# Top-k attention and a two-layer network on one core: the mask's ReLUs, GpSimd's joins and the end keys' transposes change places within a step

## The chip, the cores and the metric

The kernel runs on one core of a Trainium2 chip. The core's engines work side by side, each through its own queue in program order: TensorE (PE, matrix products and transposes; its weight loads are listed as PEld), VectorE (DVE), ScalarE (ACT), GpSimd (POOL) and SyncE (SP), whose queue issues nearly all DMAs. An instruction waits at the head of its engine's queue until the semaphores that it needs have come, and everything behind it waits too. The time is that of one execution on the device, in microseconds; lower is better. Three runs of the kernel before gave 1617.61, 1620.12 and 1620.48 us, median 1620.12.

## What is computed

Attention that keeps, for each query, only the 32 largest of 576 scores, then a normalised two-layer network with a residual, on 8 batches, 8 heads, 576 positions and head dimension 64. The weights of the network come as 64-bit floats.

```python
scores = scale * np.matmul(q, k.transpose(0, 1, 3, 2))
kth = np.partition(scores, -top_k, axis=-1)[..., -top_k:-top_k + 1]
scores = np.where(scores >= kth, scores, -1000000000.0)
attn = np.exp(scores - np.max(scores, axis=-1, keepdims=True))
attn = attn / (np.sum(attn, axis=-1, keepdims=True) + 1e-09)
x = np.matmul(attn, v)                      # heads side by side: (8, 576, 512)
mu = np.mean(x, axis=-1, keepdims=True)
var = np.mean((x - mu) ** 2, axis=-1, keepdims=True)
xn = (x - mu) / np.sqrt(var + 1e-06) * g_ln
out = x + np.maximum(xn @ w_ch1, 0.0) @ w_ch2   # 512 -> 2048 -> 512
```

## The kernel before

**Units.** The heads are taken in pairs. A unit is 128 queries of one pair: two tiles of 128 x 576 scores, one for each head. The last 64 of the 576 queries make a rest unit: one tile, with the two heads one above the other. There are 160 units, 32 of them rest units. A group is the two or three units of one job (batch, head pair, query tiles) that share a product with the values.

**Steps.** The main loop runs over steps n = 0 to 166, and in one step parts of several units are issued, so that a unit passes through five or six steps. In step n:

- PE makes the scores of unit n+2 (`scores`, `score_half`, L402) into four PSUM buffers of the pool `ps` (two for a rest unit); ACT copies them to SBUF (L383, tile `sc`).
- DVE selects in unit n (`select`, L431 to L445): the 576 columns were folded into 288 maxima and 288 minima (`halve`, L423 and L424, at the end of the step before); four rounds of eight largest find the 32nd largest.
- ACT masks unit n-1: two small instructions prepare bias and edge (`prepare`, L457 and L458), then for each of the two tiles a steep ReLU of edge minus score (L494), from which POOL subtracts the score (L497). Both write the tile `e`, of which there are two buffers. A masked place is now huge, and the exponential (`weigh`, L505, ACT) of its negative is zero.
- The exponentials are turned so that keys lie on partitions: units that are not the last of their group by DVE in blocks and by DMA through HBM (`move`, L536, unit n-2), the others by PE (`turn`, L563). The 64 keys per head that do not fill a block of 128, the end keys, are always turned by PE (`turn_ends`, L596, for rest units L592 and L593): for a moved unit three steps after its selection, n-3. That transpose is the last reader of `e`, so unit n-1's ReLU, which takes the same buffer, waits for it.
- PE multiplies a finished group with the values (`values`, L629 and L636), ACT copies (`take_values`, L644), PE transposes back (`place`, L671), ACT scales into the rows x (L648).

**Places in PSUM.** The pool `ps` has five buffers in rotation, for scores, transposes and value products alike; a new tile waits until the fifth before it has been read out. The network's products have three buffers of their own.

**The network.** Its work stands in a list `todo` and is dealt out by `fill()`, called some eight times in a step, by costs written into the program, not by what the chip does: hidden products (L776, ReLU at L799 on ACT) and second products (L815 for the first block, L933 for the others). The other blocks use seven products in place of eight on quarters of the matrices, for which POOL adds and subtracts quarters of the hidden values (L863 to L869) and, once, of the second weight matrix. These are the forms: four pairs (`form_pair`, L987 to L990, four tensor operations each), written to HBM (`keep_pair`), and fetched from there (L1003). They begin when the first block is done (`plain_done`), one pair a step; second products of the other blocks may be dealt out in steps after the one in which the last pair was kept (`formed`).

**Converting the weights.** In steps -1 to 20 the 32 pieces of 128 x 512 64-bit numbers become 32-bit: one or two pieces a step, four ahead of step 0. `split`: ACT takes size, low bits and sign (L163, L165, L168), POOL clamps the size (L164) and scales signs of the first matrix by the gain (L170). `shift` (DVE, L176) moves the size's bits. `join` (POOL, L182 and L184) adds the low bits and multiplies by the sign. The pieces split in one step are shifted and joined in the next; a piece may be used from the step after its join.

**The note.** `watch` (POOL, L464) notes whether eight minima were enough for each unit. Where they were not, a second program follows; here it doesn't run.

**Order in a step, before.** Program order, which is each engine's queue order:

1. scores of n+2 with ACT's copies, values of a group, maxima round 0;
2. the first half of the weights' work, a `fill()`, the end keys' transpose of n-3, `prepare` and the first tile's mask of n-1, a `fill()`, the second tile's mask (in steps 0 to 8 both masks come before the weights and the exponentials right behind);
3. copies of values and of end keys, transposes, rounds 1 to 3, exponentials, four more `fill()`;
4. after round 3: the note of unit n, halving of n+1, shifts and joins of the pieces split in step n-1, splits of step n, a pair of forms.

Of the kernel before, what the change touches and what calls it, by code (L numbers as in the profile page):

```python
# [29 lines left out]
def compute(  # L30
# [67 lines left out]
    def turned():  # L98
        return brief("tp")
# [110 lines left out]
    def weights(n, phase):  # L210

        now, before = batches.get(n, []), batches.get(n - 1, [])
        coming = batches.get(n + 1, [])
        if phase == 0:
            for x in coming if n < LATE else []:
                x.fetch()
            for x in now[0::2] if n < LATE else []:
                x.split()  # L220
        elif phase == 1:
            for x in before:
                x.shift()
            for x in before:
                x.join()
            for x in now if n >= LATE else now[1::2]:
                x.split()
            for x in coming if n >= LATE else []:
                x.fetch()

    todo = []
    share = [0.0]
# [143 lines left out]

    def scores(u):

        u.sc = scpool.tile([P, 2, S], FP32, tag="sc", name="sc")
        made = [score_half(u, s) for s in range(2)]  # L380
        for t in range(len(u.tiles)):
            for s in range(2):
                nc.scalar.copy(  # L383
                    u.sc[:, t, s * HALF : (s + 1) * HALF], made[s][t][:, 0:HALF]
                )

    def score_half(u, s):
# [23 lines left out]
    def halve(u):  # L411

        nt = len(u.tiles)
        u.lo = lopool.tile([P, 2, HALF], FP32, tag="lo", name="lo")
        u.hi = hipool.tile([P, 2, HALF + 8 * low_rounds], FP32, tag="hi", name="hi")  # L420
        a, b = u.sc[:, 0:nt, 0:HALF], u.sc[:, 0:nt, HALF:S]
        lo, hi = u.lo[:, 0:nt], u.hi[:, 0:nt, 0:HALF]
        nc.vector.tensor_tensor(hi, a, b, ALU.max)  # L423
        nc.vector.tensor_tensor(lo, a, b, ALU.min)  # L424
# [158 lines left out]
        heads = () if u.moved else range(len(u.tiles))  # L583
        return [lambda t=t: part(t) for t in heads] + [last]

    def turn_ends(u):

        q0 = place_of(u) * 32
        g = u.group
        ps = turned()  # L590
        if u.rest:
            nc.tensor.transpose(ps[0:R, 0:P], u.e[:, 0, JP:S], ident[:])  # L592
            nc.tensor.transpose(ps[:, P : 2 * P], u.e[:, 0, JP - R : S], ident[:])  # L593
        else:
            ends_e = u.e[:].rearrange("p t n -> p (t n)")[:, JP : JP + P]
            nc.tensor.transpose(ps[:, 0:P], ends_e, ident[:])  # L596

        def copy():
            if u.rest:
                for h in range(2):  # L600
                    nc.scalar.copy(  # L601
                        g.pt[h * R : (h + 1) * R, 2 * J, q0 : q0 + R],
                        ps[h * R : (h + 1) * R, h * (P + R) : h * (P + R) + R],
                    )
            else:
                nc.scalar.copy(g.pt[:, 2 * J, q0 : q0 + P], ps[:, 0:P])

        return copy
# [494 lines left out]
    def at(i):  # L1103
        return units[i] if 0 <= i < N else None
# [94 lines left out]
    nc.sync.dma_start(grow[:], g_ln.rearrange("(c p) -> c p", p=P))  # L1199
    load(fresh[1], nc.sync, nc.scalar)  # L1200
    scores(units[0])
    halve(units[0])
    scores(units[1])
    load_gain()
    weights(-1, 0)
    weights(-1, 1)
    for n in range(END):
# [20 lines left out]
        if quick:  # L1228
            values(g)
            take_values(g)  # L1230
        for x in ahead:
            scores(x)
        if g and not quick:
            values(g)
        if n in brings:
# [14 lines left out]
        if doubt is not None and at(n - 2) and at(n - 2).ends_watch:  # L1250
            settle_watch(at(n - 2).half)
            if n == N + 1:
                tell()
        if early:
            prepare(ex)
            for t in range(2):
                mask(ex, t)
            weights(n, 0)
            for t in range(2):
                weigh(ex, t)  # L1260
        if not early:
            weights(n, 0)
        fill()
        turned_before = at(n - 3)
        if turned_before and turned_before.moved:
            late_ends = turn_ends(turned_before)
        if mk and not early:
            prepare(mk)
            mask(mk, 0)
        fill()  # L1270
        if mk and len(mk.tiles) > 1 and not early:
            mask(mk, 1)
        if g and not quick:
            take_values(g)
        if late_ends:
# [17 lines left out]
                load(fresh[later], nc.sync, nc.sync, n >= EARLY)  # L1293
        if n == 0:
            scores(units[2])
        for x in (u if n < EARLY else None, mk if n > EARLY else None):
            if x and x is units[x.job.last]:
                load_values(x.job)
                ends_due[n + 1] = x.job
# [33 lines left out]
        fill()  # L1333
        if u:
            select(u, 3)
            if doubt is not None:
                watch(u)
        if nxt:
            halve(nxt)
        weights(n, 1)  # L1340
        if g and not quick and g.job.hp == NHP - 1:
            for qt in g.qts:
                if qt < J:
                    arrived(n, (g.job.b, qt), xs[g.job.b, qt])
        if plain_done[0] is not None and plain_done[0] < n:
            if made_pair:
                keep_pair(made_pair.pop())
            if pairs_left:
                made_pair.append(form_pair(pairs_left.pop(0)))
        if late and late.job.hp == NHP - 1:  # L1350
            r = late.job.b // 2
            if r % 2:
# [61 lines left out]
```

## Time and profile before

| | |
|---|---|
| three runs, median (lowest to highest) | 1620.12 us (1617.61 to 1620.48) |
| profiled execution: its own time, its span | 1619.01 us, 1617.1 us |
| PE, matmuls | 1482.7 us busy (92%), 7770 instructions |
| DVE | 1411.5 us (87%), 3971 |
| ACT | 1072.8 us (66%), 2984 |
| POOL | 1071.2 us (66%), 1489 |
| mean granted TensorE clock | 0.971 |
| subtractions L497 on POOL | 288, mean 1466 ns |
| ReLUs L494 on ACT | 288, mean 769 ns |
| score copies L383 on ACT | 576, mean 408 ns |
| halving L423 and L424 on DVE | 160 each, mean 967 and 1030 ns |

Busy shares are means over the whole span. An engine can be busy while another is what the end waits for, and the stretches of the run differ: until about 21 steps in, weights are converted; then the forms are made; then attention and the network run together; and at the end only the network is left. The profile counts two matmul rows for each product of the program (L776: 2304 rows).

### The profile page before, as it was taken

What the parts mean: (1) busy time and instruction counts of PE and PEld (TensorE: products, weight loads), DVE (VectorE), ACT (ScalarE), POOL (GpSimd) and SP (SyncE); (2) the same over time, 40 slices, a digit from 0 to 9 for tenths busy, and PEclk for the clock granted to TensorE, in tenths of its full rate; (3) what the DMA queues carried; (4) which work ended last, traced back from release to release, by engine and by line L of the source; (5) the groups of instructions that cost most, each with busy time, mean ns of one, the idle gap of its engine ahead of it and who ended that gap; (6) DMA issues with size and microseconds to landing.
All of it is one profiled execution on the core that took longest, in us unless ns stands there. A gap on an engine that the chain in (4) does not pass through costs nothing.

```text
span 1617.1 us, 27069 instructions
## 1 busy us (share of the span) xinstructions
PE 1482.7 (92%) x7770; PEld 1119.5 (69%) x7770; DVE 1411.5 (87%) x3971; ACT 1072.8 (66%) x2984; POOL 1071.2 (66%) x1489
## 2 busy tenths in 40 slices
PE   3568778699979999999999999999999999999997
PEld 1336446467757677777777777777777777778886
DVE  7979888999999999999999999999999999991000
ACT  5877776477767786776766867677667776754221
POOL 6768886766646666677765758576757675746244
PEclk9879999899989999999999999999999999999999
DMA  8424664544646556545564556545555555522211
GB/s 205 123 70 137 174 164 125 156 125 130 182 130 180 154 151 171 161 150 134 163 188 137 140 148 176 162 126 170 146 173 149 136 154 162 164 83 86 73 33 54
DMA packets 367205, 228.27 MB, mean 141 GB/s; under 512 B 248772, under 2 KB 337352, under 8 KB 367048
## 3 DMA queue, kind: packets, MB, share of 16 engines
q1 hardware_dynamic: 362312, 225.86, 49.1%
q8 instruction: 64, 1.05, 0.3%
q10 hardware_dynamic: 4736, 0.59, 0.2%
q14 instruction: 93, 0.76, 0.2%
HBM read 154.01 MB, written 72.35 MB: 140 GB/s over the span
## 4 chain that ended last, share of the span: by engine, by line
PE 70%; POOL 10%; DVE 9%; ACT 6%; DMA 2%; issue 1%; SPq 0%; ACTq 0%; POOLq 0%; DVEq 0%
PE hps L776 26%; PE ops L933 22%; PE scps L402 8%; PE av L629 6%; POOL e L497 3%; DVE m L445 3%; DVE hi L431 2%; PE tp L563 2%; PE av L636 2%; POOL w L184 2%; POOL wt L182 1%; ACT e L494 1%; ACT e L505 1%; ACT sc L383 1%; DVE sc L536 1%
## 5 line engine op out<-in xcount | busy, mean ns | idle before, releaser
L497 POOL TENSOR_TENSOR e<-e,sc 128x576 f32<-128x576 f32 x288 | 417.0, 1466 | 366.9 <-ACT e L494 366.6
L776 PE MATMUL hps<-xT,w 128*128 128x256 f32 x2304 | 550.9, 387 | 13.8 <-ACT xT L738 9.0
L776 PEld LDWEIGHTS hps<-xT,w 128*128 128x128 f32 x2304 | 427.8, 193 | 91.5 <-issue 16.5
L445 DVE MAX8 m<-hi 128x8 f32<-128x296 f32 (+1 forms) x1152 | 469.9, 442 | 0.1
L431 DVE MATCH_REPLACE8 hi<-m,hi 128x288 f32<-128x288 f32 (+1 forms) x864 | 377.2, 441 | 0.0
L933 PE MATMUL ops<-w,h 128*128 128x256 f32 x1360 | 326.0, 384 | 8.9 <-DMA w<-forms 7.8
L505 ACT ACTIVATE e<-e,m 128x576 f32<-128x576 f32 x288 | 224.6, 780 | 129.1 <-POOL e L497 127.6
L933 PEld LDWEIGHTS ops<-w,h 128*128 128x128 f32 x1360 | 250.2, 192 | 52.1 <-issue 8.7
L494 ACT ACTIVATE e<-sc,m 128x576 f32<-128x576 f32 x288 | 211.9, 769 | 91.8 <-PE tp L596 91.5
L383 ACT COPY sc<-scps 128x288 f32<-128x288 f32 x576 | 198.4, 408 | 89.8 <-PE scps L402 57.9
L424 DVE TENSOR_TENSOR lo<-sc 128x576 f32<-128x576 f32 (+1 forms) x160 | 164.9, 1030 | 0.0
L423 DVE TENSOR_TENSOR hi<-sc 128x576 f32<-128x576 f32 (+1 forms) x160 | 154.7, 967 | 8.9 <-ACT sc L383 4.8
L799 ACT ACTIVATE h<-hps 128x512 f32<-128x512 f32 x144 | 85.6, 595 | 96.7 <-PE hps L776 96.2
L629 PE MATMUL av<-pt,vb 128*64 128x256 f32 (+2 forms) x1088 | 142.3, 404 | 2.8 <-ACT pt L601 2.1
L536 DVE STREAM_TRANSPOSE sc<-e 128x512 f32<-128x512 f32 x176 | 114.7, 685 | 31.5 <-POOL e L497 18.9
L933 PE MATMUL ops<-wt,s 128*128 128x256 f32 x544 | 130.1, 381 | 0.0
L402 PE MATMUL scps<-kT,late_qT 64*128 64x288 f32 (+3 forms) x832 | 122.5, 411 | 1.4 <-ACT x L648 1.1
L437 DVE MAX8 hi<-lo 128x8 f32<-128x288 f32 x288 | 117.5, 443 | 0.0
L402 PE MATMUL scps<-kT,qT 64*128 64x288 f32 x512 | 95.1, 467 | 21.5 <-DVE qT L332 11.8
L629 PEld LDWEIGHTS av<-pt,vb 128*64 128x64 f32 x1088 | 72.2, 139 | 59.7 <-issue 12.8
L933 PEld LDWEIGHTS ops<-wt,s 128*128 128x128 f32 x544 | 99.1, 190 | 16.5 <-issue 3.1
L563 PE MATMUL tp<-ident,e 128*128 128x128 f32 x448 | 72.8, 290 | 40.6 <-ACT e L505 40.4
(104 smaller groups left out, 1852.0 us busy)
## 6 DMA issues: line engine op xcount, KB each, us to landing
turned<-sc SPq DMA_DIRECT2D x88, 512.0 KB, 2.9
pt<-turned SPq DMA_DIRECT2D x352, 128.0 KB, 2.8
w<-forms SPq DMA_DIRECT2D x136, 256.0 KB, 4.2
vb<-in_v_dram SPq DMA_DIRECT2D x68, 288.0 KB, 3.9
raw<-in_moe_w_ch_dram SPq DMA_DIRECT2D x32, 512.0 KB, 5.1
kT<-kept SPq DMA_DIRECT2D x36, 288.0 KB, 3.3
kin<-in_k_dram SPq DMA_DIRECT2D x128, 72.0 KB, 2.7
kept<-kT SPq DMA_DIRECT2D x32, 288.0 KB, 3.1
```

Source lines behind the costliest of these rows:

```text
L383: nc.scalar.copy(u.sc[:, t, s * HALF : (s + 1) * HALF], made[s][t][:, 0:HALF])
L402: nc.tensor.matmul(ps[i * R : i * R + ql, o : o + width], qT[r, q0 : q0 + ql], kT[r, k0 : k0 + width], start=True, stop=True,)
L423: nc.vector.tensor_tensor(hi, a, b, ALU.max)
L424: nc.vector.tensor_tensor(lo, a, b, ALU.min)
L431: nc.vector.match_replace(x, m[:, t, :], x, LOWEST)
L445: nc.vector.max(m[:, t, :], u.hi[:, t, 0:width])
L494: nc.scalar.activation(u.e[:, t], u.sc[:, t], AF.Relu, bias=u.edge[:, t : t + 1], scale=-STEEP)
L497: nc.gpsimd.tensor_tensor(u.e[:, t], u.e[:, t], u.sc[:, t], ALU.subtract)
L505: nc.scalar.activation(u.e[:, t], u.e[:, t], AF.Exp, bias=u.bias[:, t : t + 1], scale=-scale, accum_out=g.den[:, col : col + 1],)
L629: nc.tensor.matmul(av[h * D : (h + 1) * D, 0 : g.nq], vb[:, h * (J + 1) + c, :], g.blocks[:, h, 0 : g.nq // 32, c, :], start=(c == 0), sto ...
L776: nc.tensor.matmul(ps[0][:, side * N : (side + 1) * N], w1[:, c, f * P : (f + 1) * P], self.xT[:, c, 0:N], start=(c == 0), stop=(c == NC - 1),
L933: nc.tensor.matmul(bank[name][:, 0:Q], a(j), rhs, start=first and j == 0, stop=(j == G - 1), skip_group_check=not first,)
```

## The change

Within a step, four things change places. The amount of arithmetic stays the same.

- The score copies are split off (`take_scores`) and stand behind the masks. Both tiles' masks, with `prepare`, stand at the step's head, right behind the scores' matmuls, in all steps.
- The end keys' transpose of unit n-3 comes right behind the scores and writes into columns 288 to 415 of the first score buffer, of which the scores use only 288, in place of a buffer of its own. Where a step makes no scores, it takes one as before.
- The shifts go from the end of step n to its head, ahead of round 0; the joins, the note (of unit n-1 now, one step later) and a pair of forms stand behind the subtractions of n-1. The condition for forms becomes `plain_done < n - 1`.
- The first half of the weights' work stands behind all of these.

```diff
         elif phase == 1:
-            for x in before:
-                x.shift()
-            for x in before:
-                x.join()
             for x in now if n >= LATE else now[1::2]:
                 x.split()
...
+    def join_weights(n):
+        for x in batches.get(n - 1, []):
+            x.join()
...
     def scores(u):
+        u.made = [score_half(u, s) for s in range(2)]
+        return u.made[0][0][:, HALF:]
+
+    def take_scores(u):
         u.sc = scpool.tile([P, 2, S], FP32, tag="sc", name="sc")
-        made = [score_half(u, s) for s in range(2)]
...
-    def turn_ends(u):
+    def turn_ends(u, ps=None):
...
-        ps = turned()
+        if ps is None:
+            ps = turned()
...
+        for x in batches.get(n - 1, []):
+            x.shift()
+        spare = None
         for x in ahead:
-            scores(x)
+            spare = scores(x)
+        turned_before = at(n - 3)
+        if turned_before and turned_before.moved:
+            late_ends = turn_ends(turned_before, spare)
+        if mk:
+            prepare(mk)
+            for t in range(len(mk.tiles)):
+                mask(mk, t)
+        join_weights(n)
+        if mk and doubt is not None:
+            watch(mk)
+        if plain_done[0] is not None and plain_done[0] < n - 1:
+            if made_pair:
+                keep_pair(made_pair.pop())
+            if pairs_left:
+                made_pair.append(form_pair(pairs_left.pop(0)))
+        for x in ahead:
+            take_scores(x)
         if g and not quick:
             values(g)
...
+        weights(n, 0)
         if early:
-            prepare(ex)
-            for t in range(2):
-                mask(ex, t)
-            weights(n, 0)
             for t in range(2):
                 weigh(ex, t)
-        if not early:
-            weights(n, 0)
         fill()
-        turned_before = at(n - 3)
-        if turned_before and turned_before.moved:
-            late_ends = turn_ends(turned_before)
-        if mk and not early:
-            prepare(mk)
-            mask(mk, 0)
         fill()
-        if mk and len(mk.tiles) > 1 and not early:
-            mask(mk, 1)
...
             select(u, 3)
-            if doubt is not None:
-                watch(u)
...
-        if plain_done[0] is not None and plain_done[0] < n:
-            if made_pair:
-                keep_pair(made_pair.pop())
-            if pairs_left:
-                made_pair.append(form_pair(pairs_left.pop(0)))
```

The calls of `scores` outside the loop's head are each followed by `take_scores`.

More of the change, by code (lines that the diff above doesn't have):

```diff
@@ L210, in weights @@
     def weights(n, phase):
-        now, before = batches.get(n, []), batches.get(n - 1, [])
-        coming = batches.get(n + 1, [])
+        now, coming = batches.get(n, []), batches.get(n + 1, [])
         if phase == 0:
@@ L383, in scores @@
                 nc.scalar.copy(
-                    u.sc[:, t, s * HALF : (s + 1) * HALF], made[s][t][:, 0:HALF]
+                    u.sc[:, t, s * HALF : (s + 1) * HALF], u.made[s][t][:, 0:HALF]
                 )
@@ L1201, in compute @@
     scores(units[0])
+    take_scores(units[0])
     halve(units[0])
     scores(units[1])
+    take_scores(units[1])
     load_gain()
@@ L1295, in compute @@
             scores(units[2])
+            take_scores(units[2])
         for x in (u if n < EARLY else None, mk if n > EARLY else None):
```

## The prediction

> **What bounds the kernel now.** I read the windows first: five stretches, columns busy us and instructions of PE, weight loads, DVE, ACT, POOL, then granted clock, DMA share, GB/s.
>
> ```profile
> 0.00:120.00 120.00, 60.08 (x260) 37.90 (x261) 98.04 (x276) 82.72 (x209) 79.77 (x93) 0.86 0.50 134
> 120.00:320.00 200.00, 160.54 (x756) 103.73 (x756) 179.75 (x463) 135.02 (x354) 161.53 (x180) 0.91 0.54 150
> 320.00:560.00 240.00, 223.04 (x1193) 163.65 (x1191) 232.65 (x675) 171.96 (x508) 148.76 (x218) 0.96 0.52 151
> 560.00:1440.00 880.00, 872.16 (x4749) 670.58 (x4750) 876.90 (x2486) 633.75 (x1800) 603.95 (x858) 1.00 0.54 153
> 1440.00:1617.00 177.00, 166.93 (x816) 143.61 (x814) 24.14 (x75) 49.33 (x116) 77.23 (x142) 0.99 0.21 63
> ```
>
> From 560 us to the end PE is full. A busy PE may hide idle time, so I also took starts: two 128x256 matmuls in a row start 216 ns apart, and summing what exceeds the usual spacing of each kind of neighbours leaves about 25 us of gaps in 560 to 1440 (12 of them among score matmuls whose spacing varies anyway), against 78, 65 and 33 us in the three stretches before. PE's work is fixed by the change, so what can be won lies in the first 560 us, some 176 us of gaps.
>
> Next the chain of waits, steps 15 and 16 (start, length, what):
>
> ```profile
> 182.99 1.25 POOL wt L182
> 184.30 1.28 POOL w L184
> 185.63 1.98 PE ops L815 x4
> 187.82 0.78 ACT e L494
> 188.68 2.78 POOL e L497 x2
> 192.20 1.23 POOL wt L182
> ```
>
> It is a ring through three engines: a join ends on POOL, PE's queued matmuls on the joined weights run, only behind them comes the end-key transpose that frees the buffer e, then ACT's ReLU, the two subtractions, and the next joins. The list of waits says the same:
>
> ```profile
> POOL e L497 <- ACT e L494: 366.6, 132, 13.0
> ACT e L494 <- PE tp L596: 91.5, 42, 6.2
> DVE wt L176 <- POOL wt L164: 9.5, 7, 3.1
> ```
>
> Most of the 366.6 us is harmless idleness of POOL; between 120 and 340 us it is 39.2 us in 12 waits, inside the ring above.
>
> Last, DVE against POOL in the timeline:
>
> ```profile
> 965.94 0.73 DVE L423 TENSOR_TENSOR hi<-sc 128x576 f32<-128x576 f32 x1
> ...
> 980.80 1.82 POOL L913 TENSOR_TENSOR o<-o,t 128x512 f32<-128x512 f32 x1
> ...
> 981.40 1.83 DVE L424 TENSOR_TENSOR lo<-sc 128x576 f32<-128x576 f32 x1
> ```
>
> A halving instruction takes 0.73 us alone and 1.83 when POOL is in a tensor operation: it waits for POOL and then runs. Over all 320 halvings that is 103 us (duration less 0.73/0.75, or 0.44 for rest units), 64 of it after 560 us, where DVE's time is not what ends last.
>
> I count a DVE step from the end of one L424 to the end of the next. For steps 10 to 28 they last 11.2, 7.9, 11.2, 12.1, 13.2, 10.6, 9.9, 11.1, 7.9, 13.5, 10.3, 12.4, 11.5, 10.2, 13.5, 10.2, 10.8, 8.1, 15.5 us.
>
> **The change part by part.** No arithmetic is added or removed; all terms are order. The base is the profiled execution: 1619.0 us, span 1617.1; the median of the runs is 1.1 higher.
>
> *Start.* The shifts of the first four weight pieces stood at the end of step 0; they now stand ahead of step 0's first maximum, on DVE's queue.
>
> ```profile
> 13.37 0.81 DVE L445 MAX8 m<-hi 128x8 f32<-128x288 f32 x2
> ...
> 19.82 0.61 POOL L164 TENSOR_SCALAR size<-size 128x512 f32<-128x512 f32 x1
> ...
> 23.03 2.90 DVE L176 TENSOR_SCALAR size<-size 128x512 uint32<-128x512 uint32 x4
> ```
>
> The fourth clamp ends at 20.43, one shift takes 0.41, so the selection starts at about 20.9 instead of 13.37: +7.5; the 2.9 at 23.03 go. Queued behind are all of unit 0 and then halve(1). **+4.6.**
>
> *Steps 1 to 8.* One shift stands at each step's head, right behind the halving. Its ReLU needs 0.4 us from the last maximum (two 0.2 us preparations overlapped) and 0.78, so the first subtraction asks for POOL's turn 1.2 us after the maximum, while the halving (1.47) still runs; the shift then finds the subtraction in front of it. The nearest row for that is L176 itself: 0.41 alone, up to 1.62. So +1.2 a step, 9.6 in eight; what goes is the halving behind joins, 7.6 us in these steps, since joins now run 4 us after the maximum. Net **+1** (bounds -4 and +8).
>
> At this point the Trainium skill speaks against the change. Its page "SBUF — State Buffer", section "Who interferes with whom", says that a DVE instruction with two SBUF inputs, and a tensor_scalar in its two-port mode, contends with GpSimd, and that the later one waits for the whole of the other. The rows agree (1.83 beside 1.82); by the rule taken to its worst, each of two shifts behind one whole subtraction of 1.4 us, the ten steps 11 to 20 would lose 14 us more and the sum below would shrink to about -5.
>
> *Step 9* (19.1 us). DVE stands still for 8.0 us in it, 5.8 of them for the first normalised rows, which hang on unit 7: its ReLU at 100.6 (behind four score copies), subtractions 101.4 to 104.4, exponentials, transposes, products until 111.1. With the ReLU right behind the maximum (about 98.8 in this trace) and no joins ahead of the subtraction, the rows come some 6.5 us earlier in the step; 1.5 of wait stays. **-6.5** (bounds -8 and -2, the latter the score copies alone, 1.4, and a little).
>
> *Steps 10 to 20* (118.9 us). The end-key transposes now follow the scores at once, so the ReLU no longer waits for the weights' matmuls; joins need no maximum of the same step and run while DVE selects. What remains is the larger of DVE's and POOL's work. In steps 12 to 20 POOL's own is 81.4 us plus 7 in which DVE holds it, DVE's own 69.7 plus a blocked shift each; taking step by step the larger gives 89, against 99.8, a gain of 10.5. Zero is the other end: the queue order subtractions, joins, clamps is on POOL a ring either way. Nearer the first, since POOL's 39 us of waiting are really there, but a ring seldom closes fully: **-8** (bounds 0 and -14). If DVE must wait for clamps (third rival), this term is the one that goes.
>
> *Steps 21 to 26.* 21 and 22 hold DVE's idle 4.0 of 23.9, PE being in a block of 21 hidden matmuls: **-2**. In 23 to 26 the forms fill POOL (42.4 of 44.7 us, forms 5.8 a step); they stay: **-1** (both together 0 to -6).
>
> *Steps 27 and 28* (23.6 us). The built order shows that the forms' gate now opens one step later: PE's 12 projections of step 27 move to step 28 (22 there). In the trace they stood at PE's head until the DMA of 314.0 to 318.5 landed, with step 27's scores, products and transposes behind them; DVE idles 5.1 in step 28. Now step 27's attention work passes first. DVE's own work in both is 16.8; PE's 22 projections last 9.5. The DMAs, keep and fetch, move with the gate on SP's queue. **-4** (0 to -7).
>
> *Steps 29 to 56.* DVE bound, blocked only 10 us; the subtraction already starts as the halving ends in most. **-3** (0 to -8).
>
> *Step 57 to the end.* PE has no gaps to give. The note of doubt (0.19 us) and the score copies move behind ReLUs; what hides the later copies is that scores are wanted by DVE a step later. One PSUM buffer less is taken per step, but the first score buffer now stays taken until the end keys are copied. **0** (bounds -5 and +25, the latter under rival two).
>
> Sum: 4.6 + 1 - 6.5 - 8 - 2 - 1 - 4 - 3 = -18.9; 1619.0 - 18.9 + 1.1 = **1601 us**.
>
> On whether PE is full, the Trainium skill's page "Trainium Kernel Development and Optimization", section "Performance Expectations", calls matmul busy time a bad measure and weight-load busy share a good one. Weight loads are busy 76% in 560 to 1440 and 81% from 1440 on, which by that rule would leave a twentieth free, 44 us or so, and a sum near -60; the starts 216 ns apart leave a few us and I go by them.
>
> **The rivals.**
>
> *1. POOL is the wall in the conversion.* For it: from 166 to 226 us the chain is almost only POOL, 10.7 us a period, near POOL's own 9 to 10. Against: DVE waits and POOL waits in the same steps. Then steps 10 to 22 give nothing: 1601 + 10 = 1611, and with half of steps 9 and 27 also lost 1616.
>
> *2. Score buffers held too long: slower.* The copies out of the scores wait for the last maximum, two ReLUs (1.56), and the first buffer also for the end-key copy: 0.4 + 1.56 + 1.5 + 0.6, 4.1 us after the maximum. PE comes to its sixth buffer of the step about 1.24 (scores) + 0.1 + 0.9 to 3.9 (matmuls) after its scores, 2.2 to 5.2. Where PE's scores start before the maximum ends by more than about 1 us, PE waits. From step 57 on PE's scores start from 3 us before to 2 after the halving's end; 40 of some 100 steps have such a buffer, and 0.75 us in each is +30: **1631**. Against: with less blocking DVE should lead, and PE's scores then come later than the maximum. It decides from 0.5 us a step on.
>
> *3. Shifts chained to clamps.* The shift now waits a step earlier for POOL's clamp (9.5 us in 7 waits already). If DVE must follow clamp, blocked shift, selection, ReLU in a row, 2 us more in each of nine steps instead of the -8: 1601 + 8 + 11 (POOL's slack takes some) = 1620, no change.
>
> *4. DVE's blocked time counts to the end.* Then a quarter of the 64 us after 560 goes too: 1585. PE's spacing speaks against it.
>
> **How the numbers follow.** Forecast 0.55 (own range 1589 to 1612), rival 1 0.17, rival 2 0.15, rival 3 0.08, rival 4 0.05. For 8 in 10 the range takes in the first rival and most of no change: 1585 to 1622. No change is within 0.2%, 3.2 us, about what three such runs can tell. Faster: 0.55 + 0.13 + 0.05 = 0.73; same: 0.04 + 0.05 = 0.09; slower: 0.15 + 0.03 = 0.18.
>
> **What would show it.** Right: the first maximum at about 21 us; step 9 near 12; 10 to 20 near 110; no ACT wait for L596's transpose behind PE's weights' matmuls; the unit-159 halving some 19 us before 1452; gaps of PE unchanged after 560. Wrong: PE waiting for score or end-key copies at transposes after 560; DVE waiting more than 15 us in all for clamps; shifts mostly at 1.6 us twice a step.

## The result, and the profile after

The changed kernel takes 1625.61 us in the median (eight runs, 1624.34 to 1627.19) against 1620.3 for the kernel before on the same chip: a ratio of 1.0033, interval 1.0021 to 1.0044. It is slower; the forecast was 1601 us, with a range of 1585 to 1622. The profiled execution has a span of 1623.1 us at a mean granted clock of 0.965 (before: 1617.1 and 0.971).

The windows of the kernel after, with the columns of the windows before (busy us and instructions of PE, weight loads, DVE, ACT, POOL; granted clock, DMA share, GB/s):

```profile
0.00:120.00 120.00, 63.31 (x282) 40.53 (x283) 97.72 (x291) 86.35 (x220) 88.69 (x96) 0.83 0.50 134
120.00:320.00 200.00, 155.67 (x758) 101.52 (x757) 172.48 (x448) 137.76 (x362) 162.95 (x188) 0.90 0.54 150
320.00:560.00 240.00, 220.38 (x1156) 162.20 (x1154) 229.05 (x676) 161.32 (x483) 134.69 (x207) 0.95 0.51 150
560.00:1440.00 880.00, 875.06 (x4738) 672.95 (x4738) 840.85 (x2471) 619.66 (x1795) 562.99 (x854) 1.00 0.53 153
1440.00:1623.00 183.00, 172.04 (x842) 147.34 (x840) 30.07 (x91) 52.88 (x126) 81.62 (x148) 0.98 0.21 65
```

PE is still full from 560 us on, and busier (875 against 872 us), though its work is the same. DVE's busy time fell by 36 us there, since POOL blocks its halvings less (840 and 846 ns in the mean of all, against 967 and 1030); that is worth nothing where PE sets the end. The blocked part of the halvings after 560 us fell from 64 to 32 us, and the time did not follow: the fourth rival is out.

From the list of waits after (who waits, for whom; us, times, longest):

```profile
POOL e L499 <- ACT e L496: 323.9, 90, 11.3
ACT e L496 <- PE scps L599: 89.0, 65, 3.1
DVE hi L425 <- POOL watched L466: 64.0, 41, 5.1
ACT sc L385 <- POOL e L499: 49.8, 25, 7.0
PE tp L565 <- ACT sc L385: 14.9, 6, 4.8
DVE wt L176 <- POOL wt L164: 14.6, 9, 3.5
DVE size L176 <- POOL size L164: 9.4, 5, 3.1
```

The lines of the code are two or three further on than before (L494 is L496, L497 is L499, L596 is L599, L464 is L466). The ReLU's longest wait for the end keys fell from 6.2 to 3.1 us, as meant. Three waits are new or grown: the halving waits 64.0 us for the note (4.0 before), score copies wait 49.8 us for subtractions (none before), and shifts wait 24.0 us for clamps (9.5).

Where the 6 us of span arose, by the prediction's steps (DVE's halvings, after less before; the last row by PE's end):

| stretch | forecast | measured |
|---|---|---|
| start, to the halving of unit 1 | +4.6 | +9.1 |
| steps 1 to 8 | +1 | -7.3 |
| step 9 | -6.5 | -7.2 |
| steps 10 to 20 | -8 | +7.0 |
| steps 21 to 26 | -3 | -2.0 |
| steps 27 and 28 | -4 | -6.2 |
| steps 29 to 56 | -3 | +6.7 |
| step 57 to the end | 0 | +5.9 |

A second count, by PE, says what became of the leads: the start of the scores of a unit in a kernel, less that in the kernel before (us, minus is earlier). I come back to its rows.

| kernel | unit 10 | 23 | 29 | 30 | 31 | 58 | 159 |
|---|---|---|---|---|---|---|---|
| changed | -5.3 | -9.8 | -9.2 | -15.4 | -2.0 | -0.5 | +6.3 |
| e1, note back | -5.8 | -8.2 | -9.9 | -14.5 | -0.7 | -2.2 | +3.5 |
| e11, note, keys | -6.0 | -8.7 | -8.3 | -12.8 | +1.6 | -1.2 | -1.2 |
| e12, note, keys, gate | -6.0 | -8.5 | -5.7 | +4.1 | +4.2 | +2.2 | +2.7 |
| e17, the same with forms loaded first | -5.5 | -9.5 | -5.0 | -5.0 | -4.9 | -6.1 | -5.7 |
| e18, the same with older slots | -5.7 | -10.5 | -6.1 | -10.1 | -10.0 | -9.9 | -10.2 |

Two things stand out: the first three kernels, which have the change's own gate for the forms, lead by 13 to 15 us at unit 30 and by little or nothing at unit 31; and from unit 58 to 159 the changed kernel loses another 7. Part of the lead at unit 30 is only order: in the kernel before, 12 second products stand ahead of that unit's scores on PE's queue, in the changed one all 22 stand behind them. The lead of unit 29, 9.2 us, is free of this.

### The profile page after: what moved, and what is told of

It is laid out like the page before. It is cut to its first block, busy times and chain, and to the rows that moved or that the text cites. A ratio compares the mean times of both kernels' runs of the same rounds, so it can differ in the third digit from the quotient of the medians.

```text
span 1623.1 us, 27069 instructions
## 1 busy us (share of the span) xinstructions
PE 1486.5 (92%) x7770; PEld 1124.5 (69%) x7770; DVE 1370.2 (84%) x3971; ACT 1058.0 (65%) x2984; POOL 1030.9 (64%) x1489
## 5 line engine op out<-in xcount | busy, mean ns | idle before, releaser
L499 POOL TENSOR_TENSOR e<-e,sc 128x576 f32<-128x576 f32 x288 | 405.1, 1425 | 421.7 <-ACT e L496 323.9
L779 PE MATMUL hps<-xT,w 128*128 128x256 f32 x2304 | 542.1, 385 | 6.0 <-ACT xT L741 3.8
L936 PE MATMUL ops<-w,h 128*128 128x256 f32 x1360 | 322.4, 384 | 3.4 <-DMA w<-forms 3.4
L936 PEld LDWEIGHTS ops<-w,h 128*128 128x128 f32 x1360 | 254.0, 193 | 41.7 <-issue 5.0
L496 ACT ACTIVATE e<-sc,m 128x576 f32<-128x576 f32 x288 | 209.3, 769 | 90.1 <-PE scps L599 89.0
L385 ACT COPY sc<-scps 128x288 f32<-128x288 f32 x576 | 187.0, 402 | 63.3 <-POOL e L499 49.8
L425 DVE TENSOR_TENSOR hi<-sc 128x576 f32<-128x576 f32 (+1 forms) x160 | 134.3, 840 | 68.4 <-POOL watched L466 64.0
L426 DVE TENSOR_TENSOR lo<-sc 128x576 f32<-128x576 f32 (+1 forms) x160 | 135.4, 846 | 0.0
L404 PE MATMUL scps<-kT,qT 64*128 64x288 f32 x512 | 91.7, 470 | 24.8 <-DVE qT L331 23.5
L404 PEld LDWEIGHTS scps<-kT,late_qT 64*128 64x128 f32 (+1 forms) x832 | 70.6, 169 | 58.0 <-issue 18.0
```

The source lines that it names most:

```text
L385: nc.scalar.copy(u.sc[:, t, s * HALF : (s + 1) * HALF], u.made[s][t][:, 0:HALF])
L404: nc.tensor.matmul(ps[i * R : i * R + ql, o : o + width], qT[r, q0 : q0 + ql], kT[r, k0 : k0 + width], start=True, stop=True,)
L496: nc.scalar.activation(u.e[:, t], u.sc[:, t], AF.Relu, bias=u.edge[:, t : t + 1], scale=-STEEP)
L499: nc.gpsimd.tensor_tensor(u.e[:, t], u.e[:, t], u.sc[:, t], ALU.subtract)
L779: nc.tensor.matmul(ps[0][:, side * N : (side + 1) * N], w1[:, c, f * P : (f + 1) * P], self.xT[:, c, 0:N], start=(c == 0), stop=(c == NC - 1),
L936: nc.tensor.matmul(bank[name][:, 0:Q], a(j), rhs, start=first and j == 0, stop=(j == G - 1), skip_group_check=not first,)
```

## The experiments

Each time is the median of its runs; each ratio is against the kernel before, run on the same chip in the same hour. Four theories stood at the start: (1) the late note makes the halving wait, (2) the late score copies hold tiles and PSUM buffers, (3) the shifts ahead of step 0, (4) the end keys' new place costs PE time. A fifth, the forms, came out of the first runs. The fences show the main lines of each edit; `...` marks lines left out.

**e1: the note back** (1622.26 us, ratio 1.0011, 0.9999 to 1.0024).

```diff
-        if mk and doubt is not None:
-            watch(mk)
...
             select(u, 3)
+            if doubt is not None:
+                watch(u)
```

> The changed kernel with one thing undone: the note of doubt stands again right behind the last maximum of its own unit, ahead of the halving. Theory 1 (the late note makes the halving wait: hi has two buffers, so the halving of unit n+1 needs the note of unit n-1, which now stands on GpSimd behind two subtractions and four joins): the 64.0 us of DVE's waits for the note go, the conversion steps 10 to 20 get shorter by 5 to 12 us, and the time falls from 1625.6 to 1610 to 1618 us. Theory 2 (the score copies behind the ReLUs are the cost): the time stays at 1623 to 1627, and ACT's waits of its score copies for the subtraction (49.8 us in 25 waits) stay. Theory 3 (the shifts at the head of step 0): time unchanged within 2 us, first maximum still at 21 us.

Of the 64.0 us of waits 6.6 were left, and the time fell by 3.4 us (the two intervals, 1.0021 to 1.0044 and this one, just touch). Theory 1 is right in kind and small in size: most of those waits cost nothing.

**e2, e3, e4: the score copies ahead of the ReLUs again** (e3 with the note back, e4 with the start's shifts back too).

```diff
         for x in ahead:
             spare = scores(x)
+            take_scores(x)
...
-        for x in ahead:
-            take_scores(x)
```

> The changed kernel with one thing undone: the score copies stand again right behind the score matmuls, ahead of the two ReLUs on ScalarE. Theory 2 (behind the ReLUs a copy takes the tile slot of the unit whose subtraction has just been ordered, so it waits for that subtraction, and PE for the score buffer): ACT's 49.8 us of such waits and PE's about 18 us of gaps behind them go, and the time falls by 4 to 10 us to 1616 to 1622. Theory 1 (the note): DVE's 64 us of waits for the note stay, the time stays within 2 us of 1625.6 or rises a little, since the ReLU comes 1.4 us later in a step.

> Both undone together, note and score copies. What stays of the change: the ReLUs and joins ahead of the selection, the shifts at the head of the step, end keys in spare score columns, the forms' gate. If both theories hold and their costs add, the time is that of the kernel before less what the forecast saw in steps 9 to 28, plus the start: 1606 to 1614 us. If only the note costs, it equals the run with the note alone put back within 2 us; if only the copies cost, the run with the copies alone.

> As the run with note and copies put back, and besides the shifts and joins of the first four weight pieces again at the end of step 0 (all later ones stay at the heads of their steps). Theory 3: the first maximum comes again at 13.4 us instead of 21, and since nothing before step 9 but DVE's own work sets the pace, 4 to 9 us of the time go. Rival: the start's loss is taken up by waits in steps 8 to 12 anyway (unit 9's halving was only 1.8 us late in the changed kernel), and the time stays within 2 us of the run without this edit.

1675.8, 1674.2 and 1676.0 us (ratios 1.0338, 1.0325, 1.0338, each within 0.0016): 50 us slower, foreseen by no theory. The waits of e2:

```profile
PEld scps L599 <- ACT sc L385: 107.1, 78, 9.4
PE scps L599 <- ACT sc L385: 76.7, 29, 8.9
```

The end keys go into spare columns of the first score buffer. With the copies issued first, the transpose waits until ACT has read that buffer, though it writes other columns: 107.1 us of waits in the weight loads, which PE's queue issues ahead of the matmuls; the 76.7 us of the matmuls lie inside the same stretches. So the spare columns demand late copies, and these runs say nothing on theory 2. e4, with the start's shifts back as well, is no faster than e3.

**e5, e6, e7: other places for the end keys**, all with the note back. In e5 their transpose stands ahead of the scores, in a buffer of its own; in e6 the value products come ahead of it, and it stays in the spare columns; in e7 score copies and transpose are both as before.

```diff
e5
+        turned_before = at(n - 3)
+        if turned_before and turned_before.moved:
+            late_ends = turn_ends(turned_before)
         for x in ahead:
-            spare = scores(x)
+            scores(x)
...
e6
             spare = scores(x)
+        if g and not quick:
+            values(g)
...
e7
         for x in ahead:
             spare = scores(x)
+            take_scores(x)
...
         fill()
+        turned_before = at(n - 3)
+        if turned_before and turned_before.moved:
+            late_ends = turn_ends(turned_before)
```

> The note put back, and the end-key transposes one place earlier, ahead of the score matmuls, in a PSUM buffer of their own. Theory 4: with PE full after 560 us, a transpose between 64-row score matmuls and 64-column value products costs a start-to-start of 258 ns where it cost 109 between hidden products; 42 such places make 6.3 us, so the time falls from the 1622.3 of the run with the note alone put back to 1614 to 1618, and the group of a transpose followed by a value product disappears from PE's starts. Rival (only the granted clock before 560 us differs, or the fifth PSUM buffer is now taken earlier and holds the value products): no change within 2 us, or up to 5 us slower.

> The note put back, and the value products issued ahead of the end-key transposes, which stay in the spare score columns and now follow the products' last full-size matmul. Theory 4 says the same 6 us gain as for the transposes ahead of the scores: 1615 to 1619. Rival: the ReLU needs the buffer that the transposes free, so it now waits for the value products too (about 1 us a step, more where these wait for their data), which costs DVE's steps before 560 us 5 to 15 us: 1620 to 1632.

> Note, score copies and end-key transposes all as in the kernel before (transposes behind the first filling matmuls, in a buffer of their own); the ReLUs at the head of ScalarE's step, the joins behind the subtractions and the shifts at the step's head stay. In the runs with the copies alone put back PE waited at each transpose for the copy out of the same buffer, which was the cost there; it goes here. Theory 2 and 4: ACT's waits of score copies for the subtraction go (49.8 us), so do the 6 us of transposes: 1610 to 1616 us. Rival (the ring of joins, PE's queued matmuls, transposes, ReLU comes back because the transposes stand behind the weights' matmuls again): 1618 to 1626 with ACT's waits for the transposes above 90 us.

1657.98, 1649.96 and 1629.64 us (1.0231, 0.0018 to either side; 1.0183, 0.0017; 1.0060, 0.0020 or less). The waits of e5, and one of e6:

```profile
PEld av L632 <- ACT sc L385: 75.2, 33, 9.9
PE av L632 <- ACT sc L385: 59.7, 32, 9.5
```

```profile
ACT e L496 <- PE scps L599: 221.2, 76, 5.4
```

In e5 transpose and scores fill the five buffers of `ps`, so the value products wait for the first score copy, which now stands behind the ReLUs: 75.2 us in the weight loads, the matmuls' 59.7 inside them. In e6 the ReLU waits for the transpose behind the products, 221.2 us against 94.0 in e1. In e7 the ReLU waits for transposes behind the weights' matmuls again (111.2 us). The change's parts hold each other up: late copies need the spare columns, and these need the transpose next to the scores.

**e8: the first shifts and joins at the end of step 0 again**, with the note back.

```diff
-        for x in batches.get(n - 1, []):
+        for x in batches.get(n - 1, []) if n else []:
             x.shift()
...
         if nxt:
             halve(nxt)
+        if n == 0:
+            for x in batches[-1]:
+                x.shift()
+            join_weights(0)
```

> The note put back, and the shifts and joins of the first four weight pieces again at the end of step 0. Theory 3: first maximum at 13.4 us instead of 21, and 4 to 9 us of the 1622.3 go: 1613 to 1618. Rival: the loss of the start is taken up in steps 8 to 12 by waits for something else, and the time stays within 2 us of 1622.3.

1622.36 us (1.0014, 1.0005 to 1.0024), equal to e1. The rival held: PE's scores of unit 3 came 8 us earlier than in e1, those of unit 6 only 0.4. Theory 3 falls.

**e9, e10: the forms' gate back** to `plain_done[0] < n` (e10 with the note back).

> The changed kernel with one thing undone: the forms may start as soon as the plain blocks are done (step less than n again instead of less than n-1), at their new place behind the joins. Theory 5 (a common clamp at 314 to 318 us): the last stores of the forms land at 310.3 us in the kernel before and at 309.5 with the note put back, the loads of the forms are issued at 314.0 and 313.7, and PE, 10 to 15 us ahead at unit 30, is level again at unit 31, since its projections wait for them. So with the gate a step earlier the loads are issued at 300 to 305 us, PE's scores of unit 31 come 6 to 11 us earlier than in the kernel before, and of the 1625.6 us 6 to 10 go: 1615 to 1620. Rival (PE is full from there on whatever the forms do, or GpSimd is late instead): loads earlier, but the time stays within 2 us.

> Note and gate both put back. Theory 5: loads of the forms at 300 to 304 us; unit 31's scores 6 to 11 us earlier than in the kernel before; the time 6 to 10 us below the 1622.3 of the note alone: 1612 to 1616, so faster than the kernel before. Rival: 1620 to 1624.

1633.83 (1.0092, 1.0077 to 1.0106) and 1629.29 us (1.0063, 1.0049 to 1.0077): 8 us more than the changed kernel and 7 more than e1; both had been expected to be faster. SyncE's queue in the kernel before, in the changed one and in e10:

```profile
310.29 0.79 SPq L996 DMA_DIRECT2D forms<-form  x2
...
314.04 1.98 SPq L1003 DMA_DIRECT2D w<-forms  x4
```

```profile
309.89 0.79 SPq L999 DMA_DIRECT2D forms<-form  x2
310.85 1.82 SPq L548 DMA_DIRECT2D pt<-turned  x4
...
313.66 1.97 SPq L1006 DMA_DIRECT2D w<-forms  x4
```

```profile
302.82 0.80 SPq L999 DMA_DIRECT2D forms<-form  x2
...
314.97 1.74 SPq L548 DMA_DIRECT2D pt<-turned  x4
...
317.71 1.97 SPq L1006 DMA_DIRECT2D w<-forms  x4
```

The stores of the last pair come 7 us earlier, but the forms' loads stand behind `pt<-turned`, the inputs of the value products. `pt` is a single buffer, so that load waits for the previous group's products, which came later here: forms whose last store had landed at 305.9 us were called for at 317.7, and PE waited 7.4 us for them (4.4 in e1).

**e11, e12: the end keys turned ahead of the scores, in the same buffer** (e11 with the note back; e12 with the gate back too).

```diff
         for x in ahead:
-            spare = scores(x)
+            spare = brief("scps")
+            if turned_before and turned_before.moved:
+                late_ends = turn_ends(turned_before, spare[:, HALF:])
+            scores(x, spare)
...
```

> The note put back, and the end-key transpose into the spare columns of the score buffer before the score matmuls of that buffer instead of after them: no further buffer, and hidden matmul, transpose, scores, value products in PE's order. Theory 4 (a transpose between 64-row score matmuls and 64-column value products costs 149 ns more than between full-size ones, 42 times after 560 us): 1622.3 less 4 to 6, so 1616 to 1619, with the group of a transpose followed by a value product gone. Rival (the extra start-to-start only moves to the transpose in front of the scores, or is covered by waits): within 2 us of 1622.3.

> Note and gate put back and the transposes ahead of the scores in the same buffer. If the costs of theories 1, 4 and 5 are separate and add: 1622.3 less 6 to 10 less 4 to 6, so 1606 to 1612. If PE's 6 us are taken back by waits: as with note and gate alone.

e11 takes 1616.22 us (0.9979, 0.9968 to 0.9991): 6.0 less than e1 and faster than the kernel before. e12 takes 1622.86 (1.0020, 1.0011 to 1.0030): 6.4 less than e10, so this term adds to the gate's. PE's timeline (start, length, what): the transpose between filling matmuls in the kernel before; then one step with value products, after and in e11:

```profile
961.44 0.27 PE L596 MATMUL tp<-ident,e 128*128 128x128 f32 x1
961.55 1.89 PE L933 MATMUL ops<-w,h 128*128 128x256 f32 x8
```

```profile
961.07 1.19 PE L404 MATMUL scps<-kT,late_qT 64*64 64x288 f32 x10
962.20 0.33 PE L599 MATMUL scps<-ident,e 128*128 128x128 f32 x1
962.45 1.95 PE L632 MATMUL av<-pt,vb 128*64 128x256 f32 x16
```

```profile
957.32 0.27 PE L599 MATMUL scps<-ident,e 128*128 128x128 f32 x1
957.52 1.20 PE L404 MATMUL scps<-kT,late_qT 64*64 64x288 f32 x10
958.64 1.95 PE L632 MATMUL av<-pt,vb 128*64 128x256 f32 x16
```

Between scores and products the transpose adds 0.25 us ahead of the products; ahead of the scores it takes 0.20, but there it replaces the switch from a filling matmul to the scores (0.31 for a matmul that ahead of its like takes 0.22), so it adds 0.11, as it did in the kernel before. Over the 42 such steps after 560 us the median start-to-start is 258 ns, against 109 before: 6.3 us, close to the 6.0 that e11 gave back. Theory 4 is shown.

**e13, e14, e16: older slots for the score copies.** In the steps whose copies took the tile slot of the unit just subtracted, one element of the new tile is written ahead of the ReLUs, so that it gets another. e13 is the changed kernel with this alone; e14 has note and end keys as in e11; e16 is e14 with the note between subtractions and joins.

```diff
+        for x in ahead:
+            if x.i - 3 >= EARLY and not units[x.i - 3].moved:
+                x.sc = scpool.tile([P, 2, S], FP32, tag="sc", name="sc")
+                nc.gpsimd.memset(x.sc[:, 0, 0:1], 0.0)
         if mk:
             prepare(mk)
```

> The changed kernel with one edit: in the steps whose score copies took the tile slot of the unit just subtracted, one element of the new tile is zeroed on GpSimd ahead of the ReLUs, so that the tile gets an older, free slot (distance 4 or more units, as in the kernel before, instead of 3); the copies stay behind the ReLUs. Theory 2: ACT's waits of score copies for the subtraction (49.8 us in 25) and PE's waits for score buffers behind them go. One of them, 6.5 us at 298 to 304 us, holds up scores, value products, the load of the products' inputs and behind it on the SP queue the loads of the forms (issued at 313.7), so these come 4 to 7 us earlier, and of 1625.6 us 5 to 9 go: 1616 to 1621. Rival (the waits lie in slack, since PE is level with the kernel before at unit 31 for another reason): 1624 to 1627.

> The note put back, transposes ahead of the scores, older slots for the score copies. Theory 2: 1616.2 (note and transposes) less 5 to 9: 1607 to 1612. Rival: 1615 to 1618.

> As the run with note, transposes and slots, but the note stands in the later step between the subtractions and the joins. Theory 1: the halving waits for the note of the unit before; behind the subtractions alone the wait is 5 us shorter than behind the joins too, so the loss against the note at its old place is 0 to 2 us. Rival (GpSimd, waiting at the old place for the last maximum 41 times, 71.6 us in all, gains by the later place): 1 to 4 us faster than it.

1625.99 (1.0060, 1.0045 to 1.0075), 1615.54 (0.9987, 0.9978 to 0.9997) and 1616.11 us (0.9995, 0.9983 to 1.0007). No gain. In e13 one wait took another's place:

```profile
ACT sc L385 <- POOL sc L1250: 43.0, 24, 8.4
POOL sc L1250 <- DMA turned<-sc: 17.3, 10, 3.6
```

The older slots are not free either: the zeroing stands in POOL's queue and waits for the DMA that still reads the tile. The 49.8 us were not removed (43.0 took their place), so theory 2 stays open. e16, level with e14, shows no harm in a late note ahead of the joins.

**e15: e14 with the gate back; e17 and e18: the forms' loads first.** e17 is e12, and e18 is e15, with the forms' first loads ahead of `pt<-turned`:

```diff
+        fetch_forms(FETCH_AGE)
         if n in brings:
             brings.pop(n)()
```

> As the run with note, transposes and slots, with the forms' gate a step earlier. With the gate and the note put back the stores of the forms ended 7 us earlier (302.8 instead of 309.5 us), but their loads were issued 4 us later (317.7), behind the loads of the value products' inputs on the SP queue, which waited for the same score copies. If that wait was the whole cost of the gate, it is now no slower than without it: 1602 to 1612. If the earlier forms cost GpSimd's and DVE's steps 23 to 27 (unit 28 came 6 us later in PE's order), it stays 5 to 8 us slower: 1613 to 1619.

> As the run with note, gate and transposes (1622.9 us, ratio 1.0020), and on the SP queue the first loads of the forms stand ahead of the loads of the value products' inputs. Theory 5 in its second form: GpSimd is full from 266 to 312 us in every kernel (25.3 of 26 and 19.4 of 20 us), so what was gained before cannot pass it unless the forms start earlier; they did with the gate (stores done at 302.8), but their loads stood behind the loads of the products' inputs, which wait for PE. With the order turned the loads are issued at 304 to 306 us instead of 313.6 to 317.7, PE does not wait for them (7.4 us before), and the ratio falls to 0.994 to 0.998. Rival (PE is held at 300 to 310 us by score copies and value products, not by the forms): loads early, but the ratio stays at 1.000 to 1.003.

> As the run with note, gate, transposes and slots (1619.6 us, ratio 1.0011), with the same turn of the SP queue. Theory 5: loads of the forms issued at 304 to 306 us instead of 313.6, PE's 7.2 us of waiting for them gone, ratio 0.993 to 0.998. Rival: 0.999 to 1.002.

e15 takes 1619.58 us (1.0011, 0.9997 to 1.0024), 4 more than e14; PE waits 7.2 us for the forms in it, against 2.9 in e14. e17 takes 1613.78 (0.9967, 0.9956 to 0.9979), 9.1 less than e12; e18 takes **1610.60 us (0.9950, 0.9935 to 0.9965)**, the fastest. SyncE's queue in e18:

```profile
302.24 0.80 SPq L1000 DMA_DIRECT2D forms<-form  x2
...
304.36 2.64 SPq L1007 DMA_DIRECT2D w<-forms  x4
310.40 1.75 SPq L549 DMA_DIRECT2D pt<-turned  x4
```

The forms are called for at 304.4 us instead of 313.7, PE no longer waits for them, and in the table of PE's leads the row of e18 keeps its 10 us from unit 30 to the end. With that hold at the forms' loads gone, the older slots are worth 3 us (e17 to e18; the intervals just overlap). Against kernels that have neither, gate and queue together are worth 2 us (e11 to e17, within the noise) and 5 (e14 to e18): much of the 9 undoes what the gate alone had cost. No run turned the queue alone. The windows from 266 to 312 us, of the kernel before, the changed one and e18:

```profile
266.00:292.00 26.00, 20.69 (x109) 14.59 (x108) 23.50 (x65) 12.07 (x34) 25.33 (x30) 0.87 0.57 154
292.00:312.00 20.00, 15.88 (x76) 11.06 (x76) 18.87 (x47) 11.92 (x35) 19.39 (x23) 0.91 0.41 133
```

```profile
266.00:292.00 26.00, 19.91 (x103) 14.88 (x102) 24.72 (x69) 14.11 (x40) 25.34 (x30) 0.87 0.56 158
292.00:312.00 20.00, 14.26 (x68) 8.95 (x66) 19.57 (x48) 12.08 (x36) 19.39 (x22) 0.83 0.42 135
```

```profile
266.00:292.00 26.00, 17.97 (x80) 12.15 (x79) 20.52 (x50) 11.77 (x33) 25.33 (x31) 0.80 0.54 151
292.00:312.00 20.00, 16.59 (x76) 11.31 (x75) 19.59 (x47) 12.44 (x36) 19.39 (x25) 0.91 0.66 205
```

POOL (the fifth pair) is busy 44.7 of 46 us in all three. With its work as it is, this stretch can only be entered earlier.

## Why the prediction was wrong

*Steps 9, 27 and 28* went as said or better: step 9 lasted 11.9 us, and the first normalised rows no longer wait (1.5 us for them where 5.8 stood).

*Start, +4.6.* Mis-sized, +9.1: the first maximum came at 21.45 us, 8.1 later, close to what was said, but "the 2.9 at 23.03" that go had stood behind the halving of unit 1 (21.06 to 23.1 in the trace before) and could not shorten the way to it; and that halving took 3.2 us instead of 2.1. Steps 1 to 8 gave 7.3 back, where the forecast had +1 (its own terms, 9.6 less 7.6, make +2). That is the start's loss made up and not a gain: in e8, where the first maximum is early again, the same steps take 1.1 us more than before, and the time is that of e1. The whole start is worth nothing.

*Steps 10 to 20, -8.* This failed outright, +7.0. The text said that DVE's waits for clamps would undo the term, under the third rival, and gave 8 in 100 to it. The traces show the rival's place; the shifts of the last 20 pieces, before and after (ns, shortest, median and longest):

```profile
L176 DVE TENSOR_SCALAR wt<-wt x20: 409/822/1624, 131.6 to 241.2; 128x512 uint32<-128x512 uint32 x20
```

```profile
L176 DVE TENSOR_SCALAR wt<-wt x20: 414/1622/1650, 116.0 to 231.8; 128x512 uint32<-128x512 uint32 x20
```

Over the whole run DVE waits 24.0 us for clamps, above the 15 named as the sign. What DVE's time in steps 10 to 20 was made of (us; where two records overlap, the overlap counts for the first):

| | before | changed | e1 |
|---|---|---|---|
| halvings | 26.3 | 15.0 | 17.5 |
| shifts | 13.4 | 22.5 | 20.0 |
| other instructions | 67.4 | 67.0 | 67.0 |
| waits for clamps | 7.7 | 14.6 | 20.6 |
| waits for the note | 0 | 6.2 | 0 |
| other waits | 4.1 | 0.6 | 0.5 |
| all | 118.9 | 125.9 | 125.6 |

So the hoped-for part came, halvings that POOL blocks less, and was outweighed by shifts that POOL blocks more and by waits for clamps. With the shift at the step's head, a clamp from the end of the step before has no step left in which to finish; on POOL the clamps in turn waited 13.1 us for ACT's splits (0.2 before; 4.4 in e1). The failing step is "What remains is the larger of DVE's and POOL's work": it left out the wait between the two. The page "SBUF — State Buffer" of the Trainium skill, section "Who interferes with whom", spoke for the longer shifts. The estimate from it at its worst was 14 us and they grew by 9.1; that the term missed by 15 in all is near 14 by chance, since waits make up the rest. The loss is in e1, e11 and e18 too (+6.8, +8.0, +7.3), so neither note nor end keys make it, and the granted clock does not (0.94 in these steps in the changed kernel and in e18, 0.93 before). The account rests on the traces alone: no run put the later shifts back.

*Steps 29 to 56, -3, after a -4 for 27 and 28.* Measured +6.7: the gain of 27 and 28 was handed back at once. The forecast added up each step's gains as if nothing stood between them and the end. But PE's projections need the forms, and the forms come through POOL, full from 266 us, and SyncE's queue. The loads are issued at 314.04 us before and 313.66 after, so whatever was gained ahead of them ended there: 9.2 us of lead at unit 29, 2.0 at unit 31. I had read both rows, POOL's 42.4 of 44.7 us and the DMA at 314.0, and took them as reasons why single steps would not change, not as a point that all earlier gains must pass. With the gate and the queue both turned the lead at unit 29 passes (e17: 5.0 us, and 4.9 at unit 31; e18: 6.1 and 10.0).

*Step 57 to the end, 0.* Measured +5.9. "PE's work is fixed by the change" was the failing sentence: the number of matmuls is, their spacing is not. The transpose between scores and products costs 149 ns more than between filling matmuls, 6.3 us in all, and e11 took 6.0 off: from unit 58 to 159 e1 loses 5.7 us and e11 nothing. The note, "0.19 us" and costed at nothing, costs 3.4 us (e1), though mostly ahead of step 57: from unit 31 to 58 the changed kernel loses 1.5 us and e1 gains 1.5. Its price was not its length but what it holds. `hi` has two buffers, so the halving of n+1 needs the note of n-1, now behind subtractions and joins of the same step. The second rival's price (30 us) was not seen in the changed kernel, but its mechanism, too few score buffers, is what e5 shows at 36 us above e1.

On PE being full: the page "Trainium Kernel Development and Optimization", section "Performance Expectations", calls weight-load busy share a good measure of how close a kernel is to roofline, and the prediction estimated from it that 76% would leave room. e11's 6 us of PE spacing came off the time one for one, so there was none to see.

Without the two costs that were shown (3.4 and 6.0) the change is worth 3 us (e11); with the forms let through and older slots, 8 (e18). That is still some 11 short of the forecast, and the largest miss left in e18 is steps 10 to 20 (+7.3 for -8).

## What to carry to other kernels

Before adding up what steps gain, look for the next point that all of it must pass, an engine that is full for a stretch or a load that comes at a fixed time, and ask whether it starts earlier too; if not, the sum up to there is nothing. Of an instruction that is moved, ask first which buffer it is the last to read and who takes that buffer next, and of a matmul, what kind of matmul its new neighbours are. When two queues feed one engine, turn both: an earlier gate alone cost 7 us, turning the queue behind it as well took 9 off, and of what was tried only the two together gained.

## What was not expected of the chip

- A full-size transpose followed by value products on 64 columns took 258 ns from start to start, followed by a full-size matmul 109; a filling matmul took 309 ns ahead of the score matmuls on 64 rows and 216 ahead of its like. Each of these changes between forms of matmul cost 90 to 150 ns, and the order of matmuls decides how many there are. The Trainium skill's page "TensorEngine Tiling (Array Packing)", section "Key Properties", says that changing the tiling mode drains TensorE, without a price. These rows fit that and would be one, though no run shows that the drain is what they measure; I had not weighed that rule.
- Writes to columns of a PSUM buffer that nobody reads still waited for the reading of its other columns (e2: 107.1 us). The page "PSUM — Partial Sum Buffer", section "PSUM bank collisions raise a hardware error", asks for guards by bank and quadrant of partitions and not by address, which this wait fits; whether the program needed it here, no run tells.
- PE's granted clock stood at 0.5 in stretches of 3.4 to 13.7 us: 13 of them before 560 us in the kernel before, 14 in the changed one, and within the 14 us ahead of each PE had once been idle for 2.3 us or more. Less idle time does not always mean less of it: up to unit 159's scores PE was idle 6.4 us less in e1 than in the changed kernel, and the clock stood at 0.5 for 13.7 us more (119.5 against 105.8).
